# Attention with queries on partitions: small score tiles, row maxima and sums on VectorE, exponentials transposed on TensorE, v stationary

## The chip, the core and the metric

The kernel runs on one core of one Trainium2 chip. The metric is device time in microseconds (us) for one launch. Three runs of the kernel before took 972.22, 972.61 and 973.15 us; the median is 972.61 us. The profile is of one more execution.

Engines: TensorE (PE; PEld is its weight load), VectorE (DVE), ScalarE (ACT), GpSimd (POOL), SyncE (SP, which issues every DMA).

## The reference

Batch 8, 8 heads, 576 positions, head size 64. Heads 0 to 3 have a local mask (32 positions back), heads 4 to 7 a strided one (same position modulo 32, not later). The attention's output is laid out as 4608 tokens of 512 features and goes through a two-layer network:

```
scores = q k^T / 8, masked with -1e9;  attn = softmax(scores);  x = attn v
h = x @ w_in                 # 4608x512 by 512x2048
g = h * erf(softplus(h))
out = g @ w_out              # 4608x2048 by 2048x512
```

The weights come as 64-bit floats and are narrowed on the chip.

## The kernel before

**The network.** The 4608 tokens are 12 chunks of 384, the 2048 hidden features 16 tiles of 128: 192 steps, called f-tiles here and numbered h_0 to h_191 (`ftile`, line 702). One f-tile is 12 matmuls of 384 columns into a PSUM bank `h` (L716; x and the weights are split in a high and a low part, three products over four blocks of features), six operations on ACT (five L724, one L754) and five on DVE (three L721, L751, L757), which end with `ghi` and `glo`, and 9 matmuls of 512 columns into the three accumulators `o0` to `o2` (L787). L757, which writes `glo`, is the last reader of `h`; there are three such banks, so a fourth f-tile can't start before the first has its `glo`. The third L721 operation, `b<-b,a` (`n6`), is the only one of the five whose two inputs are both tensors in SBUF.

**The weights.** 32 tiles of 128x512 are loaded once (512 KB each as 64-bit words), narrowed by three DVE operations (L667, L674, L680) and split by one of ACT (L685) and one of DVE (L688) (`weight`, line 649).

**The attention.** Batches 0 and 1 go through `piece` (line 245), batches 2 to 7 through `quad` (line 415), six quads a batch. Scores stand with keys on partitions and queries along the free axis: 64x64 tiles of TensorE, four at a time, 96 query columns (local) or 126 (strided) (L484; the last strided quad takes the whole array, L474). Because the keys are on partitions, the maximum and the sum over keys go across partitions: GpSimd's partition_all_reduce does both (L516, L537). DVE adds the mask (L502), subtracts the maximum (L522), brings the sums into place by 32x32 transposes and inverts them (L552, L555, L563, L567, L571), scales the result (L587) and writes its low part (L611); ACT copies the scores to SBUF (L510), takes the exponentials (L531) and writes the high part (L606). The second product has the exponentials as moving operand and v as stationary one (L581). In batches 0 and 1 the mask is added by a TensorE matmul with the identity (L297), and in batch 0 the maximum is subtracted the same way (L317); `warm` (L900) are matmuls without use that fill PE until h_0.

**The order.** Every operation is an `Op` with an engine, a duration, a key and what it needs. `Plan.order` places them one by one on a modelled clock (least key among those that can start soonest) and writes them out in that order; nothing is reordered later, so each engine works through its own fixed list and waits where its next instruction isn't ready. The keys come from a table of constants at the top (PRO, SLOT, QE, QO, QD, ...). Loads are ops of the engine SP and stand in one queue.

Of the kernel before, what the change touches and what calls it, by code (L numbers as in the profile page):

```python
# [8 lines left out]
F32 = mybir.dt.float32  # L9
# [4 lines left out]
ALU = mybir.AluOpType  # L14
# [14 lines left out]
PRO = 77.527284  # L29
SLOT = 7.8508793  # L30
MM2 = 14.182093
W1K = (5.8795, 47.4887, -5.03539, 64.8451)
W1S = (6.27419, 16.914, 11.8133, 26.1391)
W2K = 64.060656
W2S = 9.859566
A0K = -3.2733586
A0S = 1.5337088
A0D = 20.718269
A1K = 105.58854
A1S = -4.8860706  # L40
A1D = -7.4824031
QE = (12.8837, 8.70905, 31.5965, 3.958)
QO = (-4.24866, 2.01025)
QD = (0.348349, 1.47267, 1.98055, 1.78394, 1.13326)
ASH = 3.2861291
ADT = 2.7338571
BACKLOG = 1.1130116

QL = 96
RB = 7  # L50
NA = S // 32
QS = RB * NA
# [31 lines left out]
class View:  # L84


    def __init__(self, buf, how, part, **sizes):
        self.buf, self.how, self.part, self.sizes = buf, how, part, sizes

    def __getitem__(self, key):  # L90
        return self.buf[:, self.part].rearrange(self.how, **self.sizes)[key]

TWO = {"n6", "sub", "bits0", "bits1", "bits2", "split_lo_w"}

FREED = {"maxi": 0.7, "total": 1.0}
# [12 lines left out]
class Plan:  # L110
# [34 lines left out]
    def order(self):  # L145
# [4 lines left out]
        while left:  # L150
# [24 lines left out]
            if e == "sp":  # L175
                free[e] = t + 0.6
                dma = max(dma, t + 0.6) + o.dur
                o.end = dma + 2.0
            else:
                o.end = free[e] = t + o.dur  # L180
                if o.locks:
                    held[e] = o.end - FREED.get(o.emit.__name__, 0.0)
# [7 lines left out]
def attention_moe(  # L190
# [4 lines left out]
    v_all: bass.AP,  # L195
# [20 lines left out]
    mask_l = con[:, : 2 * QL].rearrange("p (b h q) -> p b h q", b=2, h=1)  # L216
    mask_s = con[:, 2 * QL : 2 * QL + QS].rearrange("p (u q) -> p u q", u=1)
    ident_b = con[:, 2 * QL + QS :]
    neg = cpool.tile([P, P], F32, name="neg")
# [25 lines left out]
    def piece(b, hp, j, key, dt, ring, pe_mask=False, pool_sub=False, early=False):  # L245

        loc = hp < 2  # L250
        nblk = 1 if (not loc and j == 2) else 2
        n = QL if loc else (QS if j < 2 else S - 4 * QS)
        units, cols = 2 * nblk, 2 * nblk * n
        pid = f"{b}_{hp}_{j}"
        qk = buf("apool", "qk", [P, WS], f"qk_{pid}")
        v = buf("apool", "v", [P, 2, 2, D + 1], f"v_{pid}")
        s = buf("ps_h", "h", [P, 512], f"s_{pid}") if early else buf("ps_a", "ps", [P, 512], f"s_{pid}")
        sm = buf("apool", "sm", [P, 512], f"sm_{pid}")
        mx = buf("apool", "mx", [P, 512], f"mx_{pid}")
        pav = buf("ps_o", f"o{hp % 2}", [P, 512], f"av_{pid}") if early else buf("ps_a", "ps", [P, 512], f"av_{pid}")  # L260
        xn_b = buf("apool", "tt", [P, 512], f"xn_{pid}")
        xn = View(xn_b, "p (u d) -> p u d", slice(0, 4 * D), u=4)
        rc = buf("apool", "r", [P, 16, 1], f"r_{pid}")
        pt = buf("ps_a", "ps", [P, 512], f"t_{pid}")

        def load_qk():
            if loc:
                yield nc.sync.dma_start(qk[:, :WL], qk_loc[b, hp, j])
            else:
                w = nblk * (2 * n + P)  # L270
                yield nc.sync.dma_start(qk[:, :w], qk_str[b, hp - 2, j, :, :w])

        def load_v():
            w = nblk * 2 * (D + 1)
            yield nc.sync.dma_start(v.tile.rearrange("p b h d -> p (b h d)")[:, :w], v_all[b, hp, j, :, :w])

        def masks():
            if loc:
                m = mask_l if j == 0 else mask_l[:, 1:2]
                return m.broadcast_to([P, 2, 2, n]), "p (b h q) -> p b h q", dict(b=2, h=2)  # L280
            return mask_s[:, :, :n].broadcast_to([P, units, n]), "p (u q) -> p u q", dict(u=units)

        def scores():
            k0, step = units * n, n if loc else P
            for blk in range(nblk):
                dst = s[:, blk * 2 * n : (blk + 1) * 2 * n]
                yield nc.tensor.matmul(  # L287
                    dst,
                    qk[:, k0 + blk * step : k0 + blk * step + P],
                    qk[:, blk * 2 * n : (blk + 1) * 2 * n],  # L290
                    start=blk == 0,
# [3 lines left out]
                if pe_mask:  # L295
                    m = (mask_l[:, int(j > 0 or blk > 0)] if loc else mask_s[:, :, :n]).broadcast_to([P, 2, n])
                    yield nc.tensor.matmul(  # L297
                        dst.rearrange("p (h q) -> p h q", h=2), ident_b, m, start=False, stop=True,
                        skip_group_check=True,
                    )  # L300

        def mask():
            src, dst = s[:, :cols], sm[:, :cols]
# [702 lines left out]
```

## Time and profile before

| | |
|---|---|
| median of 3 runs | 972.61 us |
| span of the profiled execution, first to last instruction | 969.5 us |
| PE busy | 944.7 us (97%) |
| DVE busy | 789.4 us (81%) |
| ACT busy | 679.0 us (70%) |
| POOL busy | 328.1 us (34%) |
| granted TensorE clock | 1.000 of full speed on average |
| from HBM, to HBM | 58.34 MB, 9.44 MB |

The page shows only the span of the profiled execution, not its time as the runs measure it; 972.61 - 969.5 leaves 3.1 us around the span. PE busy counts each matmul to its modelled end, so neighbours overlap: a step is read from one start to the next. In the chain that ended last PE has 70%, DVE 18%, ACT 8%.

### The profile page before, as it was taken

The numbers are of one execution on the slowest core, as the hardware profiler recorded it, in microseconds if no ns is written. First come the engines' busy times: TensorE is split into PE (matmuls) and PEld (weight loads), VectorE is DVE, ScalarE is ACT, GpSimd is POOL, SyncE is SP. The second block draws the span as 40 slices with busy tenths as digits, with TensorE's granted clock in tenths as the row PEclk, the third lists the DMA queues.
The fourth block names the chain that finished last, engine by engine and source line by source line (L and its number), as shares of the span: only waits on it lengthen the run. The fifth ranks groups of instructions, "written<-read, shape, count | busy, mean of one in ns | idle before, by whom it ended". The sixth has DMA issues, their size and how long they took to land.

```text
span 969.5 us, 16714 instructions
## 1 busy us (share of the span) xinstructions
PE 944.7 (97%) x6056; PEld 823.7 (85%) x6056; DVE 789.4 (81%) x1727; ACT 679.0 (70%) x1541; POOL 328.1 (34%) x160
## 2 busy tenths in 40 slices
PE   8999999999999999999999999999999999999998
PEld 6788797888888888888888888888887888899997
DVE  6999999787888888887888888877788888666664
ACT  4777677767767667767767766776766766766765
POOL 3544123414535443343534444441453444000000
PEclk9999999999999999999999999999999999999999
DMA  8994202111212122112111302211221210000000
GB/s 303 337 353 140 69 1 77 37 42 57 78 37 77 46 57 68 47 38 74 46 56 38 102 21 72 77 37 45 66 65 38 88 35 15 33 1 1 33 1 33
DMA packets 37667, 68.87 MB, mean 71 GB/s; under 512 B 4176, under 2 KB 18640, under 8 KB 37584
## 3 DMA queue, kind: packets, MB, share of 16 engines
q1 hardware_dynamic: 37584, 67.80, 21.6%
q8 instruction: 48, 0.79, 0.3%
q14 instruction: 35, 0.29, 0.1%
HBM read 58.34 MB, written 9.44 MB: 70 GB/s over the span
## 4 chain that ended last, share of the span: by engine, by line
PE 70%; DVE 18%; ACT 8%; issue 2%; DMA 1%; SPq 0%; DVEq 0%
PE h L716 32%; PE o L787 29%; DVE a L721 4%; DVE b L721 4%; ACT b L724 4%; ACT a L724 2%; PE x L581 2%; DVE glo L757 2%; DVE h L751 2%; PE s L287 2%; PE s L484 1%; PE warm L900 1%; PE av L330 1%; DVE s L502 1%; ACT ghi L754 1%
## 5 line engine op out<-in xcount | busy, mean ns | idle before, releaser
L787 PE MATMUL o<-pair,ghi 128*128 128x512 f32 x1152 | 363.3, 397 | 0.0
L716 PE MATMUL h<-xhi,pair 128*128 128x384 f32 x1536 | 305.5, 341 | 15.4 <-DVE glo L757 15.3
L716 PEld LDWEIGHTS h<-xhi,pair 128*128 128x128 f32 x1536 | 266.4, 188 | 38.6 <-DVE glo L757 30.5
L724 ACT ACTIVATE b<-b 128x384 f32<-128x384 f32 x384 | 200.6, 525 | 80.0 <-DVE b L721 70.8
L787 PEld LDWEIGHTS o<-pair,ghi 128*128 128x128 f32 x1152 | 209.8, 188 | 42.0 <-issue 3.0
L516 POOL PARTITION_ALL_REDUCE mx<-sm x66 | 102.0, 1584 | 400.5 <-ACT sm L510 397.1
L787 PE MATMUL o<-pair,glo 128*128 128x512 f32 x576 | 224.8, 390 | 0.0
L537 POOL PARTITION_ALL_REDUCE su<-sm x66 | 180.7, 2780 | 32.3 <-ACT sm L531 29.4
L716 PE MATMUL h<-xlo,pair 128*128 128x384 f32 x768 | 164.5, 336 | 0.0
L721 DVE SCALAR_TENSOR_TENSOR a<-a,h 128x384 f32<-128x384 f32 x192 | 105.3, 548 | 57.7 <-ACT b L724 57.0
L724 ACT ACTIVATE a<-a 128x384 f32<-128x384 f32 x192 | 100.8, 525 | 73.1 <-DVE a L721 71.4
L721 DVE SCALAR_TENSOR_TENSOR b<-b,a 128x384 f32<-128x384 f32 x192 | 136.1, 709 | 1.8
L716 PEld LDWEIGHTS h<-xlo,pair 128*128 128x128 f32 x768 | 136.0, 188 | 0.0
L751 DVE TENSOR_TENSOR h<-b,h 128x384 f32<-128x384 f32 x192 | 106.6, 555 | 32.3 <-ACT b L724 31.7
L721 DVE SCALAR_TENSOR_TENSOR a<-h,a 128x384 f32<-128x384 f32 x192 | 105.7, 550 | 29.6 <-ACT a L724 27.9
L757 DVE TENSOR_TENSOR glo<-h,ghi 128x384 fp32r<-128x384 f32 x192 | 105.6, 550 | 28.4 <-ACT ghi L754 27.0
L787 PEld LDWEIGHTS o<-pair,glo 128*128 128x128 f32 x576 | 108.1, 188 | 23.7
L724 ACT ACTIVATE a<-h 128x384 f32<-128x384 f32 x192 | 93.1, 485 | 38.4 <-PE h L716 37.2
L754 ACT CAST ghi<-h 128x384 fp32r<-128x384 f32 x192 | 90.6, 472 | 32.8 <-PE o L787 19.8
L724 ACT ACTIVATE b<-a 128x384 f32<-128x384 f32 x192 | 100.1, 521 | 2.7
L313 POOL PARTITION_ALL_REDUCE mx<-sm x24 | 45.8, 1920 | 58.0 <-ACT sm L305 38.4
L531 ACT ACTIVATE sm<-sm 128x384 f32<-128x384 f32 (+2 forms) x66 | 36.4, 551 | 25.6 <-DVE sm L522 25.6
(54 smaller groups left out, 719.4 us busy)
## 6 DMA issues: line engine op xcount, KB each, us to landing
qk<-qk_loc SPq DMA_DIRECT2D x48, 304.0 KB, 3.1
qk<-qk_str SPq DMA_DIRECT2D x32, 380.0 KB, 3.7
v<-v_all SPq DMA_DIRECT2D x80, 130.0 KB, 2.2
out<-ob SPq DMA_DIRECT2D x36, 256.0 KB, 2.1
words<-w_in SPq DMA_DIRECT2D x16, 512.0 KB, 6.0
words<-w_out SPq DMA_DIRECT2D x16, 512.0 KB, 6.6
qk<-qk_str SPq DMA_DIRECT2D x16, 136.0 KB, 2.8
v<-v_all SPq DMA_DIRECT2D x16, 65.0 KB, 2.0
```

Source lines behind the costliest of these rows:

```text
L287: yield nc.tensor.matmul(dst, qk[:, k0 + blk * step : k0 + blk * step + P], qk[:, blk * 2 * n : (blk + 1) * 2 * n], start=blk == 0, stop=n ...
L313: yield nc.gpsimd.partition_all_reduce(mx[:, :cols], sm[:, :cols], P, ReduceOp.max)
L516: yield nc.gpsimd.partition_all_reduce(mx[k][:, :cols], sm[k][:, :cols], P, ReduceOp.max)
L531: yield nc.scalar.activation(d, d, AF.Exp, scale=1.0 / D**0.5)
L537: yield nc.gpsimd.partition_all_reduce(su[k][:, :cols], sm[k][:, :cols], P, ReduceOp.add)
L716: yield nc.tensor.matmul(ph[:, :CH], win[4 * s + cc][:, w, fs], x[cc][:, c0 : c0 + CH], start=(i == 0), stop=(i == len(terms) - 1))
L721: yield nc.vector.scalar_tensor_tensor(out=out, in0=in0, scalar=scalar, in1=in1, op0=op0, op1=op1)
L724: yield nc.scalar.activation(dst, src, func, bias=bias[i], scale=scale)
L751: yield nc.vector.tensor_tensor(out=ph[:, :CH], in0=bb.tile, in1=ph[:, :CH], op=ALU.mult)
L754: yield nc.scalar.copy(ghi.tile, ph[:, :CH])
L757: yield nc.vector.tensor_tensor(out=glo.tile, in0=ph[:, :CH], in1=ghi.tile.bitcast(F32), op=ALU.subtract)
L787: yield nc.tensor.matmul(po.tile, g[:, ts], wout[f][:, w], start=(f == 0 and i == 0), stop=(f == NFC - 1 and i == 2),)
```

## The change

`piece` and `quad` are replaced by `heads` (b, hp): one call works on two heads of one batch over all 576 positions, 4 calls a batch, 32 in all. Scores now stand with queries on partitions. A local call splits the queries in 18 blocks of 32, each against its 64 keys (40 matmuls of 64x32 array tiles with some blocks repeated, 64 columns); a strided call takes 11 blocks of 54 queries (24 matmuls of 64x64 tiles, 64 columns). The scores of a call fill two PSUM banks (2 x 320 or 2 x 384 columns). Maxima and sums are DVE reductions along the free axis. The reciprocal of the sum is multiplied into the exponentials on GpSimd, the only work left there. TensorE transposes the exponentials (6 transposes of 128x128 a call), ACT copies them to SBUF, and v is stationary in the second product (36 or 22 matmuls of 32 or 54 columns). In batch 0 ACT takes exponentials and sums in one, 64 columns at a time (`exp_sum`).

The PSUM buffer of the attention is now one pair of banks (`"ps": 1` of [128, 2, 512]) that scores, transposes and the second product of all calls from batch 1 on use in turn; before it was two single banks. Buffers for q and k, and for v, are one each instead of two and three. The table of constants has other numbers.

```
-PRO = 77.527284
-SLOT = 7.8508793
+PRO = 74.154117
+SLOT = 8.3314687
...
-TWO = {"n6", "sub", "bits0", "bits1", "bits2", "split_lo_w"}
+TWO = {"n6", "norm", "bits0", "bits1", "bits2", "split_lo_w"}
...
-    bufs = {"qk": 2, "v": 3, "sm": 3, "mx": 2, "tt": 2, "ps": 2, "h": 3, "a": 2, "b": 2, "ghi": 2, "glo": 2,
-            "ob": 3, "r": 2}
+    bufs = {"qk": 1, "v": 1, "sm": 2, "pt": 2, "mx": 2, "r": 2, "ps": 1, "h": 3, "a": 2, "b": 2, "ghi": 2, "glo": 2,
+            "ob": 3}
...
-    def piece(b, hp, j, key, dt, ring, pe_mask=False, pool_sub=False, early=False):
+    def heads(b, hp, key, dt, ring, before=(), pe_mask=False, pool_norm=True, act_sum=False, banks=None, home=None):
...
+                todo = [(t, j, h, 32) for t in range(5) for j in range(4) for h in range(2)]
+            else:
+                todo = [(t, j, h, 64) for t in range(6) for j in range(2) for h in range(2)]
+            for t, j, h, m in todo:
...
                 yield nc.tensor.matmul(
+                    bank(s, h)[m * j : m * (j + 1), 64 * t : 64 * (t + 1)],
+                    queries(rows, q0, m),
+                    keys(rows, q0),
...
-            yield nc.gpsimd.partition_all_reduce(mx[:, :cols], sm[:, :cols], P, ReduceOp.max)
...
+                yield nc.vector.tensor_tensor(out=d, in0=d, in1=m, op=ALU.add)
...
+                yield nc.vector.tensor_reduce(
+                    out=mx[:, parts[i], :units], in_=wide(of(s, i)), axis=mybir.AxisListType.X, op=ALU.max
+                )
...
                 yield nc.vector.tensor_tensor(
+                    out=wide(sm[:, parts[i]]), in0=wide(of(s, i)), in1=spread(mx, i), op=ALU.subtract
                 )
...
+                        yield nc.scalar.activation(
+                            sm[:, h, 64 * u : 64 * u + 64], bank(s, h)[:, 64 * u : 64 * u + 64], AF.Exp,
+                            bias=mx[:, h, u : u + 1], scale=1.0 / D**0.5, accum_out=rc[:, h, u : u + 1],
+                        )
...
+                yield nc.vector.tensor_reduce(
+                    out=rc[:, parts[i], :units], in_=wide(sm[:, parts[i]]), axis=mybir.AxisListType.X, op=ALU.add
+                )
...
+                yield (nc.gpsimd if pool_norm else nc.vector).tensor_tensor(out=d, in0=d, in1=spread(rc, i), op=ALU.mult)
...
+                        yield nc.tensor.transpose(bank(t, h)[:, 128 * w : 128 * w + 128], sm[:, h, c : c + 128], ident)
...
+                yield nc.scalar.copy(pt[:, parts[i]], of(t, i)[:, :, :384])
...
+                todo = [(m, a, h) for a in range(10) for m in range(2) for h in range(2) if m or a < 8]
+            else:
+                todo = [(m, a, h) for a in range(6) for m in range(2) for h in range(2) if not m or a < 5]
...
+                    px[h * D : (h + 1) * D, m, a * n : (a + 1) * n],
+                    values(rows, (2 * a + h) * D),
+                    pt[rows, h, c : c + n],
...
-    def quad(b, loc, j, key, dt, ring):
...
-                yield nc.gpsimd.partition_all_reduce(su[k][:, :cols], sm[k][:, :cols], P, ReduceOp.add)
...
+                done, _ = heads(b, hp, PRO + SLOT * (slot + ASH), ADT * SLOT, ring)
```

What stands on three engines at three places, before and now. In the names, the numbers behind a tile's name are batch, pair of heads and part; the last one counts buffers.

GpSimd, the first attention of batch 2. Before, two quads (`mx` maxima, `su` sums):

```order
L516 ISA mx_2_0_0_1857<-sm_2_0_0_1578 128x384
L516 ISA mx_2_0_0_1883<-sm_2_0_0_1579 128x384
L537 ISA su_2_0_0_1903<-sm_2_0_0_1578 128x384
L537 ISA su_2_0_0_1935<-sm_2_0_0_1579 128x384
L516 ISA mx_2_0_1_2119<-sm_2_0_1_2061 128x384
L516 ISA mx_2_0_1_2131<-sm_2_0_1_2062 128x384
L537 ISA su_2_0_1_2162<-sm_2_0_1_2061 128x384
L537 ISA su_2_0_1_2186<-sm_2_0_1_2062 128x384
```

Now all of batch 2 and the first call of batch 3 (`sm` exponentials, `r` reciprocals of the sums):

```order
L418 TENSOR_TENSOR sm_2_0_1517<-sm_2_0_1517,r_2_0_2204 128x2x320
L418 TENSOR_TENSOR sm_2_1_2160<-sm_2_1_2160,r_2_1_2306 128x2x320
L418 TENSOR_TENSOR sm_2_2_2453<-sm_2_2_2453,r_2_2_2609 128x768
L418 TENSOR_TENSOR sm_2_3_2967<-sm_2_3_2967,r_2_3_3116 128x768
L418 TENSOR_TENSOR sm_3_0_3048<-sm_3_0_3048,r_3_0_3253 128x2x320
```

A batch has 4 GpSimd instructions where it had 22, and both tensor inputs of each are in SBUF.

SP's queue at the start. Before, from the first weight tile to the third (`words` are weight tiles, `qk` and `v` the attention's):

```order
L661 DMA words8_89<-w_in 128x1024
L268 DMA qk_0_0_0_91<-qk_loc 128x608
L275 DMA v_0_0_0_93<-v_all 128x260
L268 DMA qk_0_1_0_95<-qk_loc 128x608
L275 DMA v_0_1_0_99<-v_all 128x260
L275 DMA v_0_0_1_102<-v_all 128x260
L661 DMA words0_109<-w_in 128x1024
L661 DMA words9_126<-w_in 128x1024
```

Now, from the first weight tile to the second:

```order
L530 DMA words8_90<-w_in 128x1024
L300 DMA qk7_0_1_92<-qk_loc 128x576
L301 DMA qk8_0_1_93<-qk_loc 128x608
L306 DMA v_0_0_104<-v_loc 128x1280
L300 DMA qk10_0_2_159<-qk_str 128x608
L301 DMA qk11_0_2_160<-qk_str 128x608
L308 DMA v_0_1_228<-v_loc 128x1024
L309 DMA qk8_0_1_93<-v_loc 128x256
L300 DMA qk13_0_3_251<-qk_str 128x608
L301 DMA qk14_0_3_252<-qk_str 128x608
L306 DMA v_0_2_281<-v_str 128x768
L530 DMA words9_302<-w_in 128x1024
```

The second weight tile has moved behind nearly all loads of batch 0: 4.9 MB stand ahead of it, where the second had 1.8 MB ahead.

PE, the second product of a call in batch 2 and what stands behind it. Before, one quad (`x` second product, `h` and `o` the network):

```order
L581 MATMUL x_2_0_1_2196<-sm0_2_0_1_2061,v1_2_0_1_1973 64x96
L581 MATMUL x_2_0_1_2196<-sm1_2_0_1_2062,v1_2_0_1_1973 64x96
L787 MATMUL o0_1_2010<-pair19_896,ghi_19_2133 128x512 x2
L787 MATMUL o0_1_2010<-pair19_896,glo_19_2141 128x512
L787 MATMUL o1_1_2018<-pair19_896,ghi_19_2133 128x512 x2
L787 MATMUL o1_1_2018<-pair19_896,glo_19_2141 128x512
L787 MATMUL o2_1_2026<-pair19_896,ghi_19_2133 128x512 x2
L787 MATMUL o2_1_2026<-pair19_896,glo_19_2141 128x512
L787 MATMUL o0_1_2010<-pair20_1080,ghi_20_2164 128x512 x2
L787 MATMUL o0_1_2010<-pair20_1080,glo_20_2167 128x512
```

Now:

```order
L585 MATMUL h_31_2692<-xlo3_83,pair15_1736 128x384
L446 MATMUL x_2_0_2712<-pt_2_0_2294,v_2_0_1500 64x32 x36
L656 MATMUL o0_1_2208<-pair27_1866,ghi_27_2656 128x512 x2
L656 MATMUL o0_1_2208<-pair27_1866,glo_27_2662 128x512
L656 MATMUL o1_1_2215<-pair27_1866,ghi_27_2656 128x512 x2
L656 MATMUL o1_1_2215<-pair27_1866,glo_27_2662 128x512
L656 MATMUL o2_1_2222<-pair27_1866,ghi_27_2656 128x512 x2
L656 MATMUL o2_1_2222<-pair27_1866,glo_27_2662 128x512
L427 MATMUL t_2_2_2775<-ident_84,sm_2_2_2453 128x128 x6
L656 MATMUL o0_1_2208<-pair28_1939,ghi_28_2685 128x512 x2
```

The next attention block, t_2_2, stands 9 matmuls of the network behind x_2_0 and writes the same pair of PSUM banks, which ACT and DVE must have emptied by then; before, the next one was further off and there was a second bank.

## Rows read from the trace of the kernel before

**Rows 1.** The page, part 1: busy time and instructions of each engine.

```profile
PE 944.7 (97%) x6056; PEld 823.7 (85%) x6056; DVE 789.4 (81%) x1727; ACT 679.0 (70%) x1541; POOL 328.1 (34%) x160
```

**Rows 2.** Stretches: length, then busy us of PE, PEld, DVE, ACT, POOL.

```profile
0.00:20.00 20.00, 16.11 (x107) 12.90 (x108) 12.76 (x24) 7.43 (x16) 6.69 (x8) 1.00 0.86 299
...
49.00:151.10 102.10, 97.35 (x610) 86.03 (x607) 100.82 (x231) 75.87 (x176) 33.66 (x17) 1.00 0.39 132
...
288.40:517.80 229.40, 225.52 (x1513) 195.73 (x1512) 191.05 (x422) 161.88 (x365) 93.62 (x44) 1.00 0.18 57
```

**Rows 3.** The chain that ended last, near the end: start us, length us, what.

```profile
930.80 4.08 PE o L787 x18
934.88 4.17 PE h L716 x24
```

**Rows 4.** Timeline of PE: first matmuls of h_0 and of h_16.

```profile
49.07 0.42 PE L716 MATMUL h<-xhi,pair 128*128 128x384 f32 x1
...
137.82 0.34 PE L716 MATMUL h<-xhi,pair 128*128 128x384 f32 x1
```

**Rows 5.** The chain again: the same place of two successive pairs of batches.

```profile
286.17 4.44 PE h L716 x24
...
515.64 4.44 PE h L716 x24
```

**Rows 6.** Timeline of PE: attention blocks, each with the matmul behind it.

```profile
180.90 1.09 PE L484 MATMUL s<-qk 64*64 64x126 f32 x32
181.92 0.50 PE L787 MATMUL o<-pair,ghi 128*128 128x512 f32 x1
...
213.48 0.89 PE L484 MATMUL s<-qk 64*64 64x96 f32 x32
214.30 0.50 PE L787 MATMUL o<-pair,ghi 128*128 128x512 f32 x1
...
171.59 0.88 PE L581 MATMUL x<-sm,v 128*64 128x96 f32 x16
172.40 0.73 PE L787 MATMUL o<-pair,ghi 128*128 128x512 f32 x2
```

**Rows 7.** Groups by line and form: count, busy us, mean ns, idle before.

```profile
L537 POOL PARTITION_ALL_REDUCE su<-sm x66 | 180.7, 2780 | 32.3 <-ACT sm L531 29.4 <-DVE tt L552 1.5 <-DVE tt L555 1.3
...
L721 DVE SCALAR_TENSOR_TENSOR b<-b,a 128x384 f32<-128x384 f32 x192 | 136.1, 709 | 1.8
...
L502 DVE TENSOR_TENSOR s<-s,con 128x384 f32<-128x384 f32 x36 | 18.8, 558 | 0.5 <-PE s L484 0.5
...
L502 DVE TENSOR_TENSOR s<-s,con 128x504 f32<-128x504 f32 x24 | 15.6, 685 | 0.0
...
L510 ACT COPY sm<-s 128x504 f32<-128x504 f32 x24 | 13.2, 575 | 0.0
...
L361 PE MATMUL t<-ident,xn 126*128 126x126 f32 x16 | 3.0, 271 | 0.0
```

**Rows 8.** Waits: engine, line waited for, us in total, times, longest.

```profile
PEld h L716 <- DVE glo L757: 30.5, 46, 2.0
...
PE h L716 <- DVE glo L757: 15.3, 29, 1.6
```

**Rows 9.** L721 by itself: `b<-b,a`, ns shortest, median, longest.

```profile
L721 DVE SCALAR_TENSOR_TENSOR b<-b,a x192: 495/551/2634, 56.7 to 959.7; 128x384 f32<-128x384 f32 x192
```

**Rows 10.** Timeline of all engines around 268 us: one such operation.

```profile
264.18 5.01 POOL L537 PARTITION_ALL_REDUCE su<-sm  x2 [0.21 <-ACT sm L531]
...
266.69 2.07 DVE L721 SCALAR_TENSOR_TENSOR b<-b,a 128x384 f32<-128x384 f32 x1
...
268.79 0.53 ACT L724 ACTIVATE b<-b 128x384 f32<-128x384 f32 x1 [1.32 <-DVE b L721]
...
269.78 0.51 DVE L757 TENSOR_TENSOR glo<-h,ghi 128x384 fp32r<-128x384 f32 x1
...
270.34 1.66 PE L716 MATMUL h<-xhi,pair 128*128 128x384 f32 x8 [1.01 <-DVE glo L757]
```

More of the change, by code (lines that the diff above doesn't have):

```diff
@@ L283, in scores @@
[L283 to L286, printed above, removed]
+                todo = [(t, j, h, 64) for t in range(6) for j in range(2) for h in range(2)]
+            for t, j, h, m in todo:
+                rows = slice(h * D, (h + 1) * D)
+                q0 = 32 * sub_block(t, j) if loc else NB * block(t, j)
                 yield nc.tensor.matmul(
[L288 to L291, printed above, removed]
+                    bank(s, h)[m * j : m * (j + 1), 64 * t : 64 * (t + 1)],
+                    queries(rows, q0, m),
+                    keys(rows, q0),
+                    start=(h, j) not in used,
@@ L294, in scores @@
                 )
-                if pe_mask:
-                    m = (mask_l[:, int(j > 0 or blk > 0)] if loc else mask_s[:, :, :n]).broadcast_to([P, 2, n])
+                used.add((h, j))
+            if pe_mask:
+                m = mask_l if loc else mask_s.broadcast_to([P, 6, 64])
+                for h in range(2):
+                    dst = bank(s, h)[:, :cols]
                     yield nc.tensor.matmul(
-                        dst.rearrange("p (h q) -> p h q", h=2), ident_b, m, start=False, stop=True,
-                        skip_group_check=True,
-                    )
@@ L518, in maxi, with run, spread, less @@
+        def maxi(i):
+            def run():
+                yield nc.vector.tensor_reduce(
+                    out=mx[:, parts[i], :units], in_=wide(of(s, i)), axis=mybir.AxisListType.X, op=ALU.max
+                )
             return named("maxi", run)
-        def sub(k):
+        def spread(r, i):
+            n = parts[i].stop - parts[i].start
+            return r[:, parts[i], :units].rearrange("p h (u k) -> p h u k", k=1).broadcast_to([P, n, units, 64])
+        def less(i):
             def run():
@@ new lines, in run, with norm, turn @@
+                yield nc.vector.reciprocal(r, r)
+            return named("invert", run)
+        def norm(i):
+            def run():
+                d = wide(sm[:, parts[i]])
+                yield (nc.gpsimd if pool_norm else nc.vector).tensor_tensor(out=d, in0=d, in1=spread(rc, i), op=ALU.mult)
+            return named("norm", run)
+        def turn(i):
+            def run():
+                for h in range(parts[i].start, parts[i].stop):
+                    for w in range(3):
+                        c = 64 * (2 * w if 2 * w + 2 <= units else units - 2)
+                        yield nc.tensor.transpose(bank(t, h)[:, 128 * w : 128 * w + 128], sm[:, h, c : c + 128], ident)
+            return named("turn", run)
```

637 lines of the change are left out of this document (229 added, 408 removed).

## The prediction

> **What bounds the kernel now.** I read the page's busy shares first: PE 97%, DVE 81%, POOL 34% [rows 1]. Then the stretches [rows 2], which separate two regimes. From 49 to 151 us DVE is busy for 100.8 of 102.1 us, so DVE sets the pace there. From 288 to 518 us DVE has 191.1 of 229.4 us and PE 225.5: PE sets the pace. Then the chain near the end, where no attention is left, for the price of the network alone [rows 3]: 24 first-layer matmuls take 4.17 us and 18 of the second 4.08, so an f-tile costs 8.25 / 2 = 4.125 us and 48 of them 198.0. The same place of two successive pairs of batches is 515.64 - 286.17 = 229.5 us apart [rows 5]. The 31.5 us between are attention on PE and waits.
>
> Attention on PE: a strided score block takes 1.02 us from its first matmul to the next of the network, a local one 0.82, a local second product 0.81 [rows 6]. With about 0.1 for changing over (an estimate: what remains between blocks and their neighbours) and the strided second product at the price of its scores, a pair of batches has 6 x 0.92 + 6 x 0.91 + 4 x 1.12 + 4 x 1.12 and about 1.9 for the two small quads: 21.8 us. 9.7 us of a pair are left, which are waits and the restarts behind them. The list of waits says on what: PE stood still 15.3 us, its weight loads 30.5, until DVE had written `glo` [rows 8], the release of an `h` bank.
>
> Why `glo` is late is seen in one operation. `b<-b,a` has a median of 551 ns, a mean of 709 and a longest of 2634 [rows 7, 9]. Around 268 us it takes 2.07 us while GpSimd sums a tile (264.18 to 269.19); ACT then waits 1.32 us for it, `glo` comes at 269.78, and PE stands still 1.01 us [rows 10]. So GpSimd, off the chain with 34%, delays DVE by 192 x (709 - 551) = 30 us, and part of that reaches PE.
>
> The Trainium skill (GPSIMD Engine Reference, 8. Key points) says that GpSimd shares its SBUF interfaces with DVE, whose instructions with two SBUF inputs contend with it; of an f-tile's five only `b<-b,a` is such. The trace agrees (median 551, longest 2634 ns).
>
> **The change part by part.**
>
> *PE, batches 2 to 7.* A pass is one of the two array passes of a float matmul; the score blocks hold 32. From 96 to 126 columns a pass goes from 0.82 / 32 = 25.6 to 31.9 ns [rows 6]: 0.21 ns a column and 5.6 ns fixed, four tiles side by side. At 64 columns that gives 18.9 ns, at 54 16.9, at 32 12.2. Local scores are 80 passes with eight tiles side by side: half of 18.9, 0.76 us, and 0.1. Strided scores, 48 passes: 0.91 + 0.1. Second products: 44 x 16.9 + 0.1 = 0.84 strided; local 72 passes, 0.88 by the line and 1.84 at 25.6 ns; I take 1.3, in the middle, because the stationary side still has 64 columns where the moving side has fallen to 32. Six transposes over the whole array go at four times the slope, 0.83 ns a column, 128 columns: 0.64 us (the 271 ns of a single one [rows 7] is its length with the tail, an upper end: 1.6). A batch: 2 x (0.86 + 0.64 + 1.3) + 2 x (1.01 + 0.64 + 0.84) = 10.6, a pair 21.2 against 21.8. So PE's work is the same within about 1 us a pair; all at 25.6 ns a pass would be far more (a rival below).
>
> *GpSimd.* 132 reductions of batches 2 to 7 at a mean of 2.78 us (the 66 sums [rows 7]) and less (the maxima) go; 24 multiplications come. No row shows one: from below it is DVE's 685 ns for 504 columns [rows 7] drawn on to 768, 0.95 us, from above the 2.78 us. I take 1.7, nearer the middle of both. A pair then has 8 x 1.7 = 14 us of GpSimd instead of 93.6 [rows 2]. `b<-b,a` loses 48 x 0.158 = 7.6 us or more in a pair now; in proportion 1.1 stays.
>
> The multiplication has two SBUF inputs itself, so it can hold DVE up as the reductions did; the same page gives 4497 ns for 2048 columns, an estimate of 1.7 us for 768, and calls GpSimd about twice as slow as DVE for such work. No run here shows it yet.
>
> *DVE, batches 2 to 7.* Mask, maximum and subtraction at 0.83 us (640 columns) or 0.97 (768) by the two L502 forms [rows 7], the sum about as much, small ones 0.4, low parts 0.9: some 4.6 and 5.2 us a call, 39 a pair with their tails. The removed ones stand for 191.1 less 48 x 2.9 (five operations of 0.55 and `b<-b,a` at 0.71) = 52 net of overlap. DVE falls from 83% to near 77% of a pair. That moves nothing by itself, since PE bounds; it leaves fewer late `glo`. ACT also has less (one copy of 768 instead of the copies of scores).
>
> *The waits.* Of the 9.7 us of a pair I let 6 go with the GpSimd collisions. What is late next: the single pair of PSUM banks. In the order above, t_2_2 stands 9 matmuls of the second layer (2.04 us) behind x_2_0. In that time ACT must write two high parts and DVE two low ones: 0.2 for the signal, about 0.45 each for three in a row, 0.2 again, 1.75 us if both are free. Nine such places in a pair have 1.4 to 2.8 us. I charge 0.25 us each: 2 us a pair. Net 4 us a pair; batches 2 to 7 are three pairs: 12 us.
>
> *The start.* Up to about 150 us DVE decides, so its sum counts. The 32 weight tiles cost the same. Attention of batches 0 and 1: before some 28 us of DVE work, now 8 reductions over one bank (0.5 each), 8 negations and 32 small ones (0.15), 4 calls of batch 1 with two reductions and a subtraction (0.9), and the low parts (0.45 x 16): 4 + 6 + 11 + 7 = 28. Nothing gained. But the second weight tile stands behind 4.9 MB where it had 1.8 ahead; at the 299 GB/s of the first 20 us [rows 2] that is 16 us where it was 6, with the first landing on top of both. DVE had done 12.8 us of work by 20 us [rows 2]; now some 8, so it is 5 us behind. It gets back 5 to 8 us of collisions, as GpSimd has 33.7 us of reductions in 49 to 151 us [rows 2]. `h_0` (49.07 us before [rows 4]) may come earlier: PE's list ahead of it has 236 filling matmuls instead of 136, but fewer of batch 0's own. It doesn't decide, since DVE has the same work behind it. h_16 stays at 137.8 [rows 4], less 1, with -6 to +8.
>
> Sum: 969.5 - 12 - 1 = 956.5 of span. With the 3.1 us that stand between span and median, 959.6: I say 960 us.
>
> **The rivals.**
>
> *A. As forecast,* 960; its own range 954 to 967.
>
> *B. The start gains too.* If the collisions cost more of the first 150 us than I count and the late weights less, h_16 is 6 to 8 us earlier. For it: DVE's 100.8 of 102.1 us [rows 2] holds every delay. Against it: the 3.1 MB more ahead of the second weight tile. 952.
>
> *C. The PSUM banks give the gain back.* The place is each block that follows another within 2.8 us of network work, nine a pair. If ACT and DVE need 1 us longer than 1.75 (they stand in fixed lists with other work, a copy of 504 columns alone takes 575 ns [rows 7]), each costs 0.7 us, not 0.25: 6.5 us a pair, 4 more than charged, times three: 972, no change. For it: one pair of banks and three uses a call. Against: DVE and ACT are freer.
>
> *D. Small passes have a floor: slower.* The place is every score block and second product. A call has 80 + 72 passes (local) or 48 + 44; a batch 488, six batches 2928. The shortest pass shown is 25.6 ns on average [rows 6]; if fewer columns or eight tiles bring nothing below it, they cost 75 us, in place of the 43 counted above (8.0 a batch less 0.8 for changing over): 32 us more, 992. It decides from about 19 ns a pass on (43 / 2928 is 14.7), where the 13 us are used up. Against it: two points on a line, with a fixed part of 5.6 ns.
>
> The Trainium skill (TensorEngine Tiling, Instruction Overhead) has this rule: about 60 cycles of overhead for each matmul, so one column costs as much as sixty. At 2.4 GHz that would be an estimated 25 ns a pass, 73 us for the six batches, about the same as D. The trace doesn't exclude it: its shortest pass is 25.6 ns, though the slope between 96 and 126 columns speaks for less.
>
> **How the numbers follow.** A 0.55, B 0.17, C 0.16, D 0.12. A measurement of this kernel tells 0.2% (1.9 us) from no change. Faster: A, B and a little of C, 0.74. Within 0.2%: half of C, 0.09. Slower: D and the rest of C, 0.17. The range has the -6 and +8 of the start, GpSimd's multiplication at up to 2.78 us (8 us of added collisions at most) and part of D: 948 to 976.
>
> **What would show it.** Right: `b<-b,a` with a mean under 600 ns; PE's waits for `glo` under half; a pair of batches 224 to 227 us long; h_16 near 137 us. Local scores under 1 us and local second products near 1.4 us a block, against 2 us and more under D. C would show as waits of `t`, `x` and `s` matmuls for `xlo` or `pt`. A late h_16 with an idle DVE between 10 and 50 us would say that the loads of batch 0 cost more than counted. The forecast is wrong if a pair takes 229 us or more, or h_16 comes after 146.

## The result and the profile after

The changed kernel takes 961.65 us, median of 4 runs (960.59 to 961.88); the kernel before took 972.88 us beside it (972.22 to 974.48). The ratio is 0.9882, interval 0.9862 to 0.9901: 11.2 us less. The forecast was 960 us.

The span went from 969.5 to 959.7 us. Cut at the first matmuls of h_16, h_48, h_96 and h_144 it splits so (us; differences are of the unrounded times):

| stretch | before | after | difference |
|---|---|---|---|
| start to h_16 | 137.8 | 145.3 | +7.5 |
| h_16 to h_48 | 150.6 | 149.5 | -1.0 |
| h_48 to h_96 | 229.5 | 224.2 | -5.2 |
| h_96 to h_144 | 229.5 | 224.2 | -5.3 |
| h_144 to the end | 222.2 | 216.5 | -5.7 |

So 17.3 us are won while PE sets the pace and 7.5 lost at the start. First matmuls of h_48, h_96 and h_144 before:

```profile
288.37 0.34 PE L716 MATMUL h<-xhi,pair 128*128 128x384 f32 x1
...
517.83 0.34 PE L716 MATMUL h<-xhi,pair 128*128 128x384 f32 x1
...
747.31 0.34 PE L716 MATMUL h<-xhi,pair 128*128 128x384 f32 x1
```

The busy shares on the page, as in [rows 1]:

```profile
PE 933.7 (97%) x8380; PEld 832.5 (87%) x8380; DVE 689.4 (72%) x1350; ACT 652.0 (68%) x1437; POOL 47.5 (5%) x40
```

The stretches of [rows 2], with two more inside the start; the number before the last two columns is the granted clock:

```profile
0.00:20.00 20.00, 15.96 (x337) 12.60 (x340) 8.11 (x27) 9.21 (x46) 3.60 (x8) 1.00 0.92 343
20.00:40.00 20.00, 19.93 (x351) 17.48 (x345) 19.79 (x44) 14.18 (x64) 4.39 (x4) 1.00 1.03 407
...
58.00:75.00 17.00, 8.20 (x143) 7.41 (x144) 16.31 (x29) 7.43 (x14) 3.72 (x2) 0.50 0.70 262
...
49.00:151.10 102.10, 83.87 (x920) 73.53 (x919) 98.68 (x190) 65.65 (x134) 6.71 (x4) 0.88 0.29 100
288.40:517.80 229.40, 229.40 (x2063) 204.70 (x2064) 161.34 (x313) 159.66 (x339) 11.68 (x9) 1.00 0.16 51
```

In the last one PE is busy throughout and DVE's share is 70% where it was 83%; GpSimd's 93.6 us are 11.7. In the start DVE is still nearly full from 20 us on (98.7 us in the stretch from 49 to 151.1 us, where it had 100.8), and in the first 20 us it did 8.1 us of work instead of 12.8. Timeline of PE, first matmuls of h_0, h_16, h_48, h_96 and h_144 (for the first two before see [rows 4]):

```profile
45.14 0.42 PE L585 MATMUL h<-xhi,pair 128*128 128x384 f32 x1
...
145.29 0.33 PE L585 MATMUL h<-xhi,pair 128*128 128x384 f32 x1
...
294.80 0.45 PE L585 MATMUL h<-xhi,pair 128*128 128x384 f32 x1
...
519.01 0.45 PE L585 MATMUL h<-xhi,pair 128*128 128x384 f32 x1
...
743.21 0.45 PE L585 MATMUL h<-xhi,pair 128*128 128x384 f32 x1
```

The waits that answer to [rows 8], and the operation of [rows 9] (now L590; ns shortest, median, longest):

```profile
PEld h L585 <- DVE glo L626: 3.1, 3, 2.3
...
PE h L585 <- DVE glo L626: 1.8, 1, 1.8
```

```profile
L590 DVE SCALAR_TENSOR_TENSOR b<-b,a x192: 547/551/1826, 55.4 to 950.0; 128x384 f32<-128x384 f32 x192
```

The waits for `glo` are nearly gone, and the median of `b<-b,a` is the same 551 ns as before. Most of its long cases went, so its mean is 578 instead of 709; eight over 0.6 us are left, each beside a multiplication of GpSimd. The attention blocks on PE, as in [rows 6], each with the matmul behind it, and the chain near the end, as in [rows 3]:

```profile
185.47 0.93 PE L320 MATMUL s<-qk 64*64 64x64 f32 x48
186.33 0.50 PE L656 MATMUL o<-pair,ghi 128*128 128x512 f32 x1
...
236.77 1.04 PE L320 MATMUL s<-qk 64*32 64x64 f32 x80
237.74 0.74 PE L656 MATMUL o<-pair,ghi 128*128 128x512 f32 x2
...
293.50 1.37 PE L446 MATMUL x<-pt,v 64*64 64x32 f32 x72
294.80 1.66 PE L585 MATMUL h<-xhi,pair 128*128 128x384 f32 x8
...
296.99 0.82 PE L427 MATMUL t<-ident,sm 128*128 128x128 f32 x6
297.57 0.70 PE L656 MATMUL o<-pair,ghi 128*128 128x512 f32 x2
...
306.14 0.91 PE L446 MATMUL x<-pt,v 64*64 64x54 f32 x44
306.98 0.50 PE L656 MATMUL o<-pair,ghi 128*128 128x512 f32 x1
```

```profile
933.31 4.18 PE h L585 x24
937.49 4.12 PE o L656 x18
```

From start to start: local scores 0.97 us, strided 0.86, second products 1.30 and 0.84, six transposes 0.58. A pair of batches then has 4 x (0.97 + 0.58 + 1.30) + 4 x (0.86 + 0.58 + 0.84) = 20.5 us, and 22.9 with 0.1 us of changeover at each of the 24 blocks; before, reckoned in the same way, it was 21.8. So the new form takes no work off PE. The network itself became slower: (4.18 + 4.12) / 2 = 4.15 us an f-tile, where it was 4.125.

### The profile page after: what moved, and what is told of

It is laid out like the page before. It is cut to its first block, busy times and chain, and to the rows that moved or that the text cites. A ratio compares the mean times of both kernels' runs of the same rounds, so it can differ in the third digit from the quotient of the medians.

```text
span 959.7 us, 20411 instructions
## 1 busy us (share of the span) xinstructions
PE 933.7 (97%) x8380; PEld 832.5 (87%) x8380; DVE 689.4 (72%) x1350; ACT 652.0 (68%) x1437; POOL 47.5 (5%) x40
## 4 chain that ended last, share of the span: by engine, by line
PE 89%; DVE 8%; issue 1%; ACT 1%; DMA 1%; SPq 0%
PE o L656 41%; PE h L585 40%; PE x L446 3%; PE s L320 2%; PE t L427 2%; DVE w L543 2%; DVE w L549 1%; DVE pair L557 1%; DMA words<-w_in 1%; DVE w L536 1%; DVE a L590 1%; ACT sm L392 1%; DVE mx L356 0%; DVE xlo L470 0%; DVE b L590 0%
## 5 line engine op out<-in xcount | busy, mean ns | idle before, releaser
L585 PEld LDWEIGHTS h<-xhi,pair 128*128 128x128 f32 x1536 | 273.9, 189 | 13.4 <-DVE glo L626 3.1
L656 PE MATMUL o<-pair,glo 128*128 128x512 f32 x576 | 226.8, 394 | 0.0
L590 DVE SCALAR_TENSOR_TENSOR a<-a,h 128x384 f32<-128x384 f32 x192 | 105.7, 550 | 87.1 <-ACT b L593 87.1
L593 ACT ACTIVATE a<-a 128x384 f32<-128x384 f32 x192 | 100.8, 525 | 80.9 <-DVE a L590 80.9
L590 DVE SCALAR_TENSOR_TENSOR a<-h,a 128x384 f32<-128x384 f32 x192 | 106.4, 554 | 41.8 <-ACT a L593 41.6
L590 DVE SCALAR_TENSOR_TENSOR b<-b,a 128x384 f32<-128x384 f32 x192 | 110.9, 578 | 2.0
L418 POOL TENSOR_TENSOR sm<-sm,r 128x768 f32<-128x768 f32 (+3 forms) x36 | 47.3, 1314 | 699.1 <-DVE r L411 546.1
L446 PEld LDWEIGHTS x<-pt,v 64*64 64x64 f32 x1848 | 32.9, 136 | 11.5 <-issue 3.6
L320 PEld LDWEIGHTS s<-qk 64*32 64x32 f32 (+1 forms) x1872 | 25.1, 121 | 17.2 <-issue 13.3
L446 PE MATMUL x<-pt,v 64*64 64x32 f32 (+1 forms) x1848 | 36.8, 223 | 1.9 <-ACT pt L433 1.8
```

Of the source, the lines that this page charges most:

```text
L320: yield nc.tensor.matmul(bank(s, h)[m * j : m * (j + 1), 64 * t : 64 * (t + 1)], queries(rows, q0, m), keys(rows, q0), start=(h, j) not in ...
L418: yield (nc.gpsimd if pool_norm else nc.vector).tensor_tensor(out=d, in0=d, in1=spread(rc, i), op=ALU.mult)
L446: yield nc.tensor.matmul(px[h * D : (h + 1) * D, m, a * n : (a + 1) * n], values(rows, (2 * a + h) * D), pt[rows, h, c : c + n], start=Tru ...
L585: yield nc.tensor.matmul(ph[:, :CH], win[4 * s + cc][:, w, fs], x[cc][:, c0 : c0 + CH], start=(i == 0), stop=(i == len(terms) - 1))
L590: yield nc.vector.scalar_tensor_tensor(out=out, in0=in0, scalar=scalar, in1=in1, op0=op0, op1=op1)
L593: yield nc.scalar.activation(dst, src, func, bias=bias[i], scale=scale)
```

## The experiments

The theory was: the gain is GpSimd's collisions with DVE, not the new form of the attention; the loss at the start has its own causes, and the 0.025 us of an f-tile another. Rivals stand with each run. Lines with + are the edits.

**GpSimd taken out of the kernel before** (e2_no_reduce).

```diff
-                yield nc.gpsimd.partition_all_reduce(mx[k][:, :cols], sm[k][:, :cols], P, ReduceOp.max)
+                yield from ()
...
-                yield nc.gpsimd.partition_all_reduce(su[k][:, :cols], sm[k][:, :cols], P, ReduceOp.add)
+                yield from ()
...
```

> The kernel before with one thing taken out: in batches 2 to 7 GpSimd's maxima and sums over partitions are left out (the subtraction takes the scores' own copy and the reciprocals are taken of the exponentials, so the attention's values change), everything else in place and in order. Theory: GpSimd was what made PE wait for glo; b<-b,a falls to 560 ns or less, PE's waits for glo from 15.3 to under 4 us, a pair of batches from 229.5 to 222 to 224 us (198.0 for the network, 21.8 for attention, 2 to 4 for the rest), and the time from 972.6 to 953 to 957 us, lower than with the change. Rival (DVE's 83% or the form of the attention makes glo late): a pair stays at 228 to 230, the time at 970 to 973 us.

952.10 us (951.38 to 952.93), ratio to the kernel before 0.9785 (0.9765 to 0.9806). Its stretch h_48 to h_96, `b<-b,a`, and the waits:

```profile
285.20:508.30 223.10, 223.10 (x1514) 196.40 (x1514) 181.81 (x421) 161.69 (x366) 0.00 (x0) 1.00 0.18 58
```

```profile
L721 DVE SCALAR_TENSOR_TENSOR b<-b,a x192: 495/550/560, 59.2 to 941.4; 128x384 f32<-128x384 f32 x192
```

```profile
PEld h L716 <- DVE glo L757: 5.5, 12, 2.0
...
PE h L716 <- DVE glo L757: 2.2, 3, 1.6
```

No `b<-b,a` is longer than 560 ns, the waits for `glo` fall from 15.3 to 2.2 us, a pair from 229.5 to 223.1, while DVE is still busy for 81% of it. The rival falls: neither DVE's load nor the form of the scores made `glo` late. The run takes away two things, the collisions and DVE's waits for GpSimd's results; the second is small, 3.4 us in the whole kernel before. The longest of them there:

```profile
DVE tt L552 <- POOL su L537: 1.4, 3, 0.5
```

**GpSimd loaded in the kernel after** (e1_pool_load).

```diff
...
+                if b > 1:
+                    for _ in range(12):
+                        yield nc.gpsimd.partition_all_reduce(extra, ident, P, ReduceOp.add)
```

> The changed kernel with GpSimd work put back: in batches 2 to 7 twelve sums over partitions of a 128x128 tile, which nobody reads, stand behind each multiplication. At an estimated 0.9 us each (the 2.78 us of before's sums, scaled by columns) GpSimd is busy some 95 to 100 us of a pair of batches, as before (93.6), where it now has 11.7; DVE, ACT and PE keep their work and order. Theory (GpSimd's collisions with DVE are what the change took away): b<-b,a goes from 578 ns to 650 or more on average, the waits of first-layer matmuls for glo come back, a pair is 4 to 6 us longer than its 224.2 us, and the time 974 to 980 us. Rival (what paid is the lighter list of DVE, 70% of a pair instead of 83%, so that a late b<-b,a no longer reaches PE): b<-b,a gets as late, but a pair stays within 1.5 us of 224.2 and the time at 962 to 966 us.

1156.23 us (1153.83 to 1157.30). Both expectations missed. `b<-b,a` is at 581 ns, as without the load: 59 of them ran beside these narrow sums at a mean of 593, where 67 beside the wide ones of before (behind 150 us) had 985. What stretched the kernel is GpSimd's own queue:

```profile
589.14 5.77 POOL L423 PARTITION_ALL_REDUCE extra<-ident  x5
601.69 1.25 POOL L420 TENSOR_TENSOR sm<-sm,r 128x640 f32<-128x640 f32 x1 [6.78 <-issue]
609.07 13.93 POOL L423 PARTITION_ALL_REDUCE extra<-ident  x12 [6.13 <-issue]
```

```profile
PE t L432 <- POOL sm L420: 167.3, 13, 19.8
```

Between a reduction and a multiplication GpSimd stands 6 to 8 us without an instruction, and the multiplication, which PE's transposes wait for, comes behind all of it. So the run says nothing on what wide reductions do in this kernel, and putting the collisions back is not shown. It shows that GpSimd's multiplication stands on PE's path: the transposes take its result, so what is queued in front of it costs PE time.

**PE's passes** (e5_scores_twice).

```diff
-            for t, j, h, m in todo:
+            for n, (t, j, h, m) in enumerate(todo * (2 if b > 1 else 1)):
+                used = set() if n % len(todo) == 0 else used
```

> The changed kernel in which batches 2 to 7 compute each block of scores twice in a row into the same place: 256 more small passes a batch, 1536 in all, nothing else new. Theory (PE sets the pace and a pass costs what the line through 96 and 126 columns gave, 9.5 ns in local and 18.9 ns in strided blocks; by the trace after the change somewhat more, 13 and 18 ns): a pair is 6.7 to 7.3 us longer, 20 to 22 us in all, 981 to 984 us. Rival D (a floor of 25 ns a pass): 38 us, 1000 us. Rival E (PE waits for others in these batches, so that more work on it is hidden): under 12 us, below 974 us.

982.23 us (981.70 to 986.11). First matmuls of h_48 and h_96:

```profile
299.72 0.45 PE L586 MATMUL h<-xhi,pair 128*128 128x384 f32 x1
...
531.84 0.45 PE L586 MATMUL h<-xhi,pair 128*128 128x384 f32 x1
```

A pair takes 232.1 us, 7.9 more; 982.23 - 961.65 = 20.6 us for 1536 passes is 13.4 ns each, 7.9 us for a pair's 512 is 15.4. All of the added work shows, so PE sets the pace (E falls), and D's 25 ns is out. The rule of the Trainium skill behind D (TensorEngine Tiling (Array Packing), Instruction Overhead) doesn't hold as a price of a pass for these small tiles side by side: by it the added passes would have cost an estimated 38 us.

**Addresses** (e3_shift, e4_shift32, and e9_before_32 on the kernel before). Each adds one unused tile behind `ident`, of 392, 8 and 8 floats per partition:

```diff
     ident = cpool.tile([P, P], F32, name="ident")
+    cpool.tile([P, 8], F32, name="shift")
```

> The changed kernel with 1568 bytes per partition left empty behind the constants, so that the tiles of the network and the weights start at the SBUF addresses of the kernel before; no instruction changes. In the stretch without attention an f-tile takes 4.154 us where it took 4.123. Theory (addresses): matmuls collide in SBUF with what ACT and DVE read and write there; at the old addresses an f-tile is back at 4.12 to 4.13 us, 192 of them give back 5 to 6 us, time 955 to 957 us. Rival (another cause, such as the instruction stream or the order of weights among the addresses): 4.15 us, 961 to 962 us.

> The changed kernel with only 32 bytes per partition left empty behind the constants: the tiles of the network and the weights then start at odd multiples of 32 bytes, as before the change and as in the run with 1568 bytes (956.06 us), but 1536 bytes lower than there. Theory (alignment): what slowed the matmuls is that these tiles start at multiples of 128 bytes; the first layer's step is back from a mean of 174.5 ns to 173.6, the second's from 228.8 to 226.8, an f-tile at 4.12 to 4.13 us, time 955 to 957 us. Rival (it matters which larger stretch of SBUF a tile lies in): the steps stay spread, time 960 to 962 us.

> The kernel before with 32 bytes per partition left empty behind the constants, so that its tiles of the network start at multiples of 64 bytes. Theory (alignment): its matmul steps spread as in the changed kernel, to means of 174.5 and 228.8 ns at the end, an f-tile goes from 4.123 to 4.15 us, and the time rises by 4 to 6 us to 977 to 979 (less where PE waits anyway). Rival (larger stretches of SBUF decide): nothing moves, 972 to 974 us.

| kernel | start of the tiles `a` to `glo` and of the weights, bytes modulo 128 | mean step, first layer, ns | second layer, ns | time, us |
|---|---|---|---|---|
| before | 32 | 173.6 | 226.8 | 972.88 |
| after | 0 | 174.5 | 228.8 | 961.65 |
| e3_shift | 32 | 173.6 | 226.8 | 956.06 (954.69 to 959.17) |
| e4_shift32 | 32 | 173.6 | 226.8 | 955.57 (954.50 to 957.59) |
| e9_before_32 | 64 | 176.6 | 226.7 | 977.02 (973.65 to 980.93) |

(Steps are from start to start of neighbouring matmuls of one layer behind 850 us.) The chain at the end of e4_shift32, then of e9_before_32:

```profile
909.98 4.17 PE h L586 x24
914.15 4.08 PE o L657 x18
```

```profile
900.40 4.24 PE h L717 x24
904.63 4.08 PE o L788 x18
```

32 bytes are enough. The ratio to the kernel before, run beside each (972.04 us), is 0.9817 (0.9793 to 0.9841) for e4_shift32 and 1.0040 (1.0021 to 1.0058) for e9_before_32. The alignment is shown as the cause of the longer steps; that e9_before_32 slowed the first layer alone, and not both as in the changed kernel, was not foreseen, and which access of another engine the matmuls meet stays open.

**The start.** First the multiplications of batches 0 and 1 left out (e6_no_norm_start).

```diff
+                if b < 2:
+                    return
```

> The changed kernel without the multiplication on GpSimd in batches 0 and 1 (the exponentials stay unscaled there), the order of all else unchanged. h_16 starts at 145.3 us, 7.5 later than before the change. Theory: a good part of that is collisions of these multiplications with DVE, which has no idle time between 20 and 140 us (seven operations there are 0.5 to 1.3 us too long, each beside one of them, 6.0 us together); without them h_16 comes 5 to 7 us earlier and the time is 955 to 957 us. Rival (the start is late for its loads and for ACT's sums alone, and DVE would wait instead): h_16 moves by less than 2 us, time 960 to 962 us.

957.01 us (955.50 to 957.83), and h_16 6.1 us earlier:

```profile
139.16 0.33 PE L587 MATMUL h<-xhi,pair 128*128 128x384 f32 x1
```

DVE's operations, 7.7 us longer in sum than undisturbed ones up to the `glo` of h_16, are 0.7 us longer here, and DVE's idle time is the same (15.4 us before 150 us, 15.5 in the changed kernel): what went are the collisions. But not all of the 6.1 us: at h_8 the run is 4.6 us earlier (102.67 for 107.30), and 1.6 us come between h_8 and h_12, from the granted clock. There PE waited 1.8 us for `glo` in the changed kernel, and from 119.3 to 122.7 us its clock was at the lower level (1.2 of 2.4 GHz). e5_scores_twice, which has the same order up to there, had the same wait but not the lower clock. 119 to 123 us of both, the changed kernel first:

```profile
119.00:123.00 4.00, 4.00 (x15) 3.70 (x13) 3.69 (x9) 2.58 (x6) 0.00 (x0) 0.57 0.00 0
...
119.00:123.00 4.00, 4.00 (x21) 3.51 (x20) 4.00 (x9) 3.23 (x7) 0.00 (x0) 1.00 0.00 0
```

From h_8 to h_12 it is 21.0 us in the changed kernel, 19.4 in e5_scores_twice and 19.5 in this run. So the collisions that the new multiplications bring are worth 4.6 to 6 us at the start. One of them in the changed kernel:

```profile
58.23 0.23 DVE L411 RECIPROCAL r<-r 128x12 f32<-128x12 f32 x1
58.37 0.63 DVE L549 SCALAR_TENSOR_TENSOR w<-words,w 128x512 uint32<-128x512 uint32 x1
58.62 1.70 POOL L418 TENSOR_TENSOR sm<-sm,r 128x768 f32<-128x768 f32 x1 [19.75 <-DVE r L411]
58.91 1.95 DVE L543 SCALAR_TENSOR_TENSOR w<-words,w 128x512 uint32<-128x512 uint32 x1
```

The last row takes 1.95 us, where it has 0.68 alone. Could the multiplications go elsewhere? On DVE (e8_norm_dve, with the 32 bytes):

```diff
+        pool_norm = b > 1
```

> The changed kernel with 32 bytes left empty (955.57 us by itself, h_16 at 142.8 us) and with the multiplications of batches 0 and 1 on DVE instead of GpSimd. Theory (a multiplication on GpSimd costs DVE about as much in collisions, 0.5 to 1.3 us each, as DVE would need to do it): the collisions of the first 80 us, 6 us, go, and 8 multiplications of 0.5 us and 4 of 0.8 to 0.9 us, some 7.5 us, come to an engine without idle time; h_16 moves by -1 to +3 us and the time is 954 to 958 us. Rival (GpSimd does take this work off DVE, and the collisions only push operations that had slack): h_16 5 us or more later, 960 us and above.

961.21 us (957.63 to 961.43), h_16 at 149.49 instead of 142.83: by these the rival. No operation of DVE is over 0.25 us too long any more, but the multiplications are added to its work, and before 150 us it is idle 18.8 us, where e4_shift32 has 13.3. But two of the five runs, 957.63 and 958.42 us, lie in the theory's range; their mean granted clock was 0.993, that of the others 0.986 to 0.989, and the profile is of one of these. That GpSimd takes this work off DVE by more than its collisions cost is likely, then, and not shown.

Then the order. e7_shift_plan moves two figures of the planner's model, with 1568 bytes left empty:

```diff
-        live, dma, left = {}, 0.0, len(self.ops)
+        live, dma, left = {}, 2.5, len(self.ops)
...
```

> The changed kernel with 1568 bytes left empty as in the run of 956.06 us, and with two figures of the planner's model moved towards the trace: the first loads land 2.5 us later (dma starts at 2.5 instead of 0) and `invert` takes 0.31 us instead of 0.25. In the first 80 us DVE runs up to 9 us behind the planned times, and GpSimd's multiplications then meet two-input operations that the plan had kept apart from them. Theory: with a plan nearer to the run fewer meet, h_16 comes 3 to 6 us earlier than in the run of 956.06 us (142.9 us) and the time is 950 to 953 us. Rival (the later loads cost as much as the collisions, or the meetings fall elsewhere): within 2 us of 956.

956.15 us (956.00 to 958.74): the rival; 6 long operations are left, of 7. e10_aware has the rule as well that keeps two-input operations of DVE off from the reciprocal on:

```diff
...
+                if o.emit.__name__ == "invert":
+                    held["pool"] = max(held["pool"], o.end + 0.25 + o.pool)
...
```

> The changed kernel with 32 bytes left empty and a planner that keeps DVE's two-input operations away from GpSimd's multiplication from the end of the reciprocal on (before, it let GpSimd begin only 0.6 us after it, or when DVE's operation had ended; the trace shows it beginning 0.2 us after it and DVE's next operation then held up), with the first loads 2.5 us later in its model as in the run of 956.15 us. The same operations stand in another order. Theory (collisions at the start are a matter of order): those of over 0.25 us before 150 us fall from 6 or 7 to 2 at most, h_16 comes at 139 to 141 us (142.8 without it) and the time is 952 to 954.5 us. Rival (DVE has nothing else ready then and waits instead): 955 to 957 us.

954.14 us (953.15 to 958.06), ratio to before 0.9816 (0.9793 to 0.9839). Long operations fall to 2, their excess from 6.1 to 1.3 us, but h_16 is at 142.25, 0.6 us earlier: DVE's idle time before 150 us rises from 13.3 to 16.6 us. The time is the theory's, the mechanism the rival's: DVE waits instead. It is the fastest version here that leaves nothing out, though not told apart from e4_shift32. With another table of constants (e11_aware_keys):

> The kernel of the run before with other numbers in the table of constants for the first two batches and the weights, found by a search on the planner's own model (attention of batch 1 later, between the first f-tiles). By that model the first 16 f-tiles end 2 us earlier for the same work; on the chip the order of loads, weights and attention decides. Theory (the start is bound by DVE's sum and by where it is idle in the first 20 us, so an order can win only the collisions and a little idle time): 950 to 954 us, h_48 at 286 to 289 us (291.6 without both). Rival (the chip departs from the model where it waits for loads): 954 to 958 us.

957.61 us (954.21 to 958.66), h_48 at 294.8: the rival; the planner's own model does not find a better start.

Last, the second weight tile ahead (e12_weights_early, with the 32 bytes):

```diff
-        op = add("sp", P * 8 * n / 3.6e5, key - 8.0, load, new=[words])
+        op = add("sp", P * 8 * n / 3.6e5, key - (8.0 if i != 9 else 20.0), load, new=[words])
```

> The changed kernel with 32 bytes left empty (955.57 us by itself; DVE idle 11.1 of the first 20 us, h_16 at 142.8 us) and the second weight tile's load directly ahead of the first, third in SP's queue instead of behind 4.9 MB. Theory (DVE starts late because the second weight tile does): DVE has 2.1 us more of the tile's work within the first 20 us, is idle 8 to 9 us there instead of 11.1, h_16 comes 2 to 3 us earlier and the time is 952.5 to 954 us. Rival (DVE waits there for batch 0's scores and for ACT's sums, whose loads now stand behind 0.5 MB more): the idle time moves behind 20 us, h_16 within 1 us, time 955 to 957 us.

956.03 us (955.03 to 961.61), h_16 at 144.15 where e4_shift32 has 142.83. The first 20 us of this run, then of e4_shift32:

```profile
0.00:20.00 20.00, 15.82 (x362) 12.69 (x363) 10.09 (x30) 9.55 (x47) 2.65 (x7) 1.00 0.91 339
...
0.00:20.00 20.00, 15.93 (x370) 13.03 (x371) 8.91 (x28) 10.09 (x52) 3.60 (x8) 1.00 0.93 341
```

DVE has 10.09 us of work there instead of 8.91: of the 2.1 us that the theory expected 1.2 came, so the late weight tile is a part of DVE's late start. But it bought no time, and there the theory falls: before 150 us ten operations of DVE are over 0.25 us too long where seven were, with 7.7 us in sum instead of 6.1, and the granted clock was at its lower level for 27.3 us instead of 20.5. The waits of DVE in the first 20 us of the changed kernel show the larger part:

```profile
DVE mx L356 <- PE s L333: 4.8, 2, 3.3
DVE con L687 <- DMA con_f<-consts: 3.6, 1, 3.6
DVE r L410 <- ACT sm L392: 2.7, 3, 1.5
DVE w L536 <- DMA words<-w_in: 0.6, 1, 0.6
```

It waits for batch 0's scores and for ACT's sums; for weight words only 0.6 us. The 3.6 us for the constants are no loss against before, where this wait was 3.4.

## Why the prediction was right, and where not

The time was right (960 for 961.65), and so was rival A's mechanism for batches 2 to 7. But two terms were off, in opposite directions, and two more, the alignment and the clock, were missing; that their sum came out within 2 us is luck in part.

- **Collisions in batches 2 to 7: right, and too small.** `b<-b,a`, the waits for `glo` and a pair of 224.2 us came as written. The part of the waits that goes was put at 6 of 9.7 us a pair, less 2 for the single pair of PSUM banks, net 4, 12 in all. It is 5.2 to 5.7 a pair even with slower matmuls; at the old alignment a pair is 223.0 us, 6.4 less. The 2 us for the banks (rival C) are not there: behind 119 us no matmul starts over 0.2 us late, behind 123 us none over 0.12, and no wait of PE is on the list behind 130 us. The 0.2 us for a signal in that sum stand in no row; operations that waited for another engine mostly started 0.03 to 0.06 us behind the end of what they waited for.
- **PE's attention: right within 1 to 2 us.** 21.2 us forecast, with 0.1 for changing over at half of the blocks; 20.5 measured from starts without it, 22.9 with it at all. Local scores 0.97 for 0.86, strided 0.86 for 1.01, the second products to the hundredth. Rival D is out by the run with doubled scores.
- **DVE in batches 2 to 7: the work right, the share not.** Its attention was put at 39 us a pair and measures 38.7 as a sum of lengths, but the share fell to 70% and not to 77%: the forecast took the old operations off net of overlap and put the new ones on in full length.
- **GpSimd's multiplication:** 1.7 us forecast for 768 columns, measured

```profile
L418 POOL TENSOR_TENSOR sm<-sm,r 128x768 f32<-128x768 f32 x14 | 21.4, 1529 | 320.7 <-DVE r L411 314.4 <-ACT pair L554 6.3
L418 POOL TENSOR_TENSOR sm<-sm,r 128x640 f32<-128x640 f32 x14 | 18.1, 1294 | 347.8 <-DVE r L411 224.6 <-PE o L656 72.4 <-ACT b L593 44.0
```

- **The start: wrong step.** "It gets back 5 to 8 us of collisions" did not happen, and rival B with it. DVE up to the `glo` of h_16 (151.1 and 157.2 us), with each record split at the first quartile of its form: work 155.2 and 158.0 us, excess 8.1 and 7.7, idle 11.3 and 15.5 (records overlap, so these sum to more than the stretch). GpSimd's reductions had cost at most 8 us there, and 12 multiplications, each with two SBUF inputs, cost as much. The prediction named this property of the multiplication and priced it in batches 2 to 7 alone. The work is 2.8 us more, not equal. With h_16 at 145.3 the forecast also came close to its own sign of being wrong, 146.
- **The 5 us of late DVE: right size, cause right only in part.** In the first 20 us it is idle 11.9 us, 4.7 longer than before, and over the whole start 4.2 longer. Most of it is for the scores and sums of batch 0; moving the second weight tile ahead brought back 1.2 us of the work and no time (e12_weights_early).
- **Not foreseen: the alignment.** 961.65 - 955.57 = 6.1 us. In the traces some 4.5 of the 7.0 us of span lie behind h_16, and these are the longer steps. The rest is at the start, where executions of the same order differ: 1.4 us of it come between h_0 and h_4, where the changed kernel's clock was at the lower level from 81.8 to 85.2 us and that of e4_shift32 was not; no run separates the two causes there.
- **Not foreseen: the clock.** Before, the granted clock was 1.00 throughout; in the changed kernel it was at the lower level for 23.9 us between 58 and 123 us. The last 3.4 of these cost 1.6 us (h_16 at 145.3, and at 143.6 in e5_scores_twice, which lacks them). What the others cost no run separates; DVE, which sets the pace there, was idle 2.2 us between 58 and 86 us, 0.4 before.

Forecast -12 - 1 = -13 us of span, measured -17.3 + 7.5 = -9.8. The term that counted on gains at the start was the weak one, and the larger gain behind it covered that.

## What to carry to other kernels

Price an engine off the chain by whose operations it holds up, and check the same property in what replaces it: here a multiplication with two SBUF inputs took over at the start just what the reductions had cost. Where DVE sets the pace, moving work off it pays only for what isn't paid back in collisions. After any change of buffers compare a stretch that the change doesn't touch; if its instructions got slower, try a shift of the tiles by 32 bytes early: here that was one line and 6 us.

## What was not expected of the hardware

- Matmul steps depend on where tiles start in SBUF: 173.6 and 226.8 ns at 32 bytes modulo 128, 174.5 and 228.8 at 0, 176.6 and 226.7 at 64, with x at the same addresses throughout.
- In e1_pool_load GpSimd stands 6 to 8 us without an instruction and without a wait that the profile shows at a change between multiplication and partition reduction: 24 places before a reduction, 5.8 to 6.2 us each, 142.7 in sum, and 13 before a multiplication, 6.8 to 8.3 us, 94.6 in sum. The Trainium skill (GPSIMD Engine Reference, 2.1 Instruction dispatch) tells of about 6 us for the first call of a freshly loaded routine, without an instruction in the profile; these gaps agree in size or are a little longer, and the change from the one to the other may be such a load each time; no run shows that it is.
- GpSimd also holds up DVE operations with one tensor input: before, `w<-words` (L667) was 0.38 to 0.83 us too long six times in the first 110 us, always beside a reduction, though seven others that met one were not; now the small `mx<-mx` at 14.16 us took 0.53 too long.
- Partition sums of 128 columns hold `b<-b,a` up by 42 ns (593 against 551), those of 384 to 504 by over 400.
- The granted clock was 0.50 of full speed, the lower of its two levels of 1.2 and 2.4 GHz, from 58 to 75 us of the changed kernel, after PE had been busy for 4.3 of the 8 us before; in the kernel before, with 15.8 us of PE work in the same 17, it was 1.00.
